# Group 8 of the tokens loaded as seven tokens on each of 64 partitions per sequence, and the unread matmuls of the drain left out

## The chip, the core and the metric

The kernel runs on one core of a Trainium2 chip. Five engines work side by side: PE (TensorE, matrix products; its weight loads are listed as PEld), DVE (VectorE), ACT (ScalarE), POOL (GpSimd) and SP (SyncE, which here only issues transfers). Sixteen DMA engines move data between the chip's main memory and the on-chip memory of 128 partitions. The metric is the time on the device of one execution, in microseconds (us); lower is better.

## What is computed

Four sequences (B = 4) of S = 5056 tokens with D = 256 channels go through a gated recurrence, and its result goes through a mixture of 8 experts with 4 slots each (32 slots in all). From the reference:

```python
sig = 1.0 / (1.0 + np.exp(-f_logit))
f = lower_bound[None, None, :] + (1.0 - lower_bound[None, None, :]) * sig
i = 1.0 - f
for t in range(S):
    h = f[:, t] * h + i[:, t] * x[:, t]
    y[:, t] = h
...
logits = x @ phi                       # x is y, all 20224 tokens
d = exp(logits - logits.max(0)); d /= d.sum(0) + 1e-09
slot_input = (d.T @ x).reshape(E, S_per_e, D)
slot_out[e] = np.maximum(slot_input[e] @ w1[e], 0.0) @ w2[e]
c = exp(logits - logits.max(1)); c /= c.sum(1) + 1e-09
out = c @ slot_out
```

The inputs x and f_logit are 20.7 MB each, the weights w1 and w2 together 16.8 MB, the output 20.7 MB. Nothing of the output can be computed before every token has gone through the recurrence and every expert's weights are there, since the softmax d runs over all tokens.

## The kernel before

**Tiling.** Each sequence is cut into 10 groups of 512 tokens. Groups 0 to 7 and the last, 9, are full; group 8 (called `odd`) has the 448 tokens that are left between 4096 and 4544. A unit is one group of one sequence: 40 units, worked off in the order of n = 0 to 39 in one loop. Units 32 to 35 are group 8 of sequences 0 to 3, units 36 to 39 are group 9.

**A unit's way through the engines.**
1. `load(n)`: SP issues the transfers of f_logit and x into tiles `f_t` and `x_t`, of two units each ([128, 2, 4, 256] in 4-byte numbers). Each kind has three buffers, so a load waits until the tile of three pairs earlier has been read.
2. `gate(n)`: ACT computes the sigmoid of the pair's `f_t` into `s_t` (2-byte numbers).
3. `enter(n)`: POOL multiplies `s_t` and `x_t` into `u_t` (L252).
4. `s_to_channels` and `u_to_channels`: PE turns `s_t` and `u_t` so that channels lie on the partitions and tokens run along them. Two channels of 2 bytes travel as one 4-byte number, so a turn is a transpose by an identity matrix.
5. `decay`: ACT makes the factors `a` out of the turned s. `scan`: DVE runs the recurrence over the tokens (two scans a unit, L319), its start value taken from the same sequence's group before.
6. `to_tokens`, `keep_tokens`: PE turns h back to tokens on partitions, DVE or ACT copies it out. `logits`, `exps`, `weights_to_tokens`, `slots`: the products with phi, the exponentials and the sums into the 32 slots.

**How a group lies on partitions.** A load must give each partition a run of consecutive tokens, for then the run is one packet of the transfer. In the first groups a partition holds 4 tokens of a unit (4096 bytes). The units from 8 to 31 are `long`: a pair of them is two successive groups of one sequence, a partition holds 8 tokens in a row (8192 bytes), and partitions 0 to 63 hold the first group, 64 to 127 the second. Such a pair's u is turned by halves, by `half_to_channels` (L273: eight transposes of 64 partitions for each unit), which reads both u tiles.

Group 8 pairs two sequences. Its 448 tokens are 3 x 128 + 64: each sequence has 3 tokens on each of 128 partitions (`R3`), and the 64 tokens that remain of both sequences share a fourth column (`rest`), token by token, sequence 0 on the even partitions and 1 on the odd ones. So a load of a pair has three transfers for f_t and three for x_t: the column (L222, 128 packets of 1024 bytes) and two blocks (L226, 128 packets of 3072 bytes each). `to_channels` turns such a unit with one product that sorts even and odd partitions apart (L261) and three transposes (L264).

**The order of the work** is written out by hand in the loop over n: at even n, `load(n + 6)`; then `gate`, `enter(n + 3)`, `to_tokens(n - 1)`, `s_to_channels` of two units, `u_to_channels(n + 1)`, `scan(n)`. Each engine does its instructions in that order. POOL also issues the transfers of the weights, which convert them to 2 bytes (`load_w`, at the places that `W_AT` lists: one each at n = 9, 17, 25, 31, 32, two at 33, three at 34, six at 36), so each stands in POOL's queue behind the `enter` before it. The transfers are taken up by the sixteen DMA engines in the order of each queue.

**The drain.** After the loop come the last group's slots, then the slots' sums are copied out by DVE (`slot_sb`), turned by PE (`sin_ps`), scaled (`sin`) and sent through the experts. At two places, after `late_slots` and after the `sin_ps` products, the kernel has PE do matmuls whose results nobody reads: `spin` (two of 128x256) and `narrow` (ten of 32x256), each time 12. Then the experts' products follow, each as its weights land (L631, L670, L728), and the output is computed in blocks and stored.

Of the kernel before, what the change touches and what calls it, by code (L numbers as in the profile page):

```python
# [9 lines left out]
F32 = mybir.dt.float32  # L10
# [8 lines left out]
def kernel(  # L19
# [10 lines left out]
    nc = tc.nc  # L30
    B, S, D = x.shape
    E = moe_w1.shape[0]
    F = moe_w1.shape[2]
    NS = moe_phi.shape[1]
    SPE = NS // E
    P = 128
    DC = D // P
    FC = F // P
    R = 4
# [6 lines left out]
    def first(g):  # L46
        return g * G if g < n_grp - 1 else S - G

    def used(g):
        return first(g + 1) - first(g) if g < n_grp - 1 else G  # L50
# [2 lines left out]
        return used(g) // R  # L53

    odd = n_grp - 2
    R3 = used(odd) // P
    L = used(odd) - P * R3
    assert 2 * L == P

    wide_r = 4 * R  # L60
    n_blk = (S // (P * wide_r))
# [1 line left out]
    blocks.append((n_blk * P * wide_r, (S - n_blk * P * wide_r) // P))  # L63
    assert sum(P * n_r for _, n_r in blocks) + L == S


    consts = ctx.enter_context(tc.tile_pool(name="consts", bufs=1))
    ident_f = consts.tile([P, P], F32, name="ident_f")
# [52 lines left out]
    rrow = store.tile([P, n_grp * R, B], F32, name="rrow")  # L121
    left = store.tile([P, L, 2], BF16, name="left")
    nc.vector.memset(left, 0.0)
# [8 lines left out]
    w1_sb = [wts.tile([P, DC, F], BF16, name=f"w1_sb{e}") for e in range(E)]  # L132
# [14 lines left out]
                nc.gpsimd.dma_start(out=w2_sb[i - E][:, ds(f, k)], in_=w2_r[i - E][:, ds(f, k)])  # L147


    def spin(dst, k, w):  # L150
        for _ in range(k):
            nc.tensor.matmul(dst[:, ds(0, w)], w1_sb[0][:, 0, :P], w1_sb[0][:, 0, :w],
                             start=True, stop=True, skip_group_check=True)

    def narrow(dst, k):
        for i in range(k):
            nc.tensor.matmul(dst[ds(i % B * NS, NS), ds(0, D)], w1_sb[0][:, 0, ds(0, NS)],
                             w1_sb[0][:, 0, ds(0, D)], start=True, stop=True,
                             skip_group_check=True)

    W_AT = {9: 1, 17: 1, 25: 1, 31: 1, 32: 1, 33: 2, 34: 3, 36: 6}
    w_next = [0]
    ctx.enter_context(tc.manual_schedule())
# [4 lines left out]
    with tc.tile_pool(name="sp2", bufs=3) as sp2, \  # L168
# [9 lines left out]
        slot_bank = pslot.tile([P, 2, D], F32, name="slot_ps")  # L178
# [12 lines left out]
        xs, fs, sts, uts, pss, psus, hs, hps, hts, lgs, ets = ({} for _ in range(11))  # L191

        def long(n):
            return 2 * B <= n < n_unit - 2 * B

        def place(n):
            if long(n):
                t, j = divmod(n, 2 * B)
                return 2 * t + j % 2, j // 2
            return divmod(n, B)  # L200
# [9 lines left out]
        def load(n, k=2):  # L210
            for src, dst, tag in ((f_logit, fs, "f_t"), (x, xs, "x_t")):
                if n % 2 == 0:
                    dst[n // 2] = ld.tile([P, 2, R, D], F32, name=tag, tag=tag)
                t = dst[n // 2]
                if long(n):
                    g, b = place(n)
                    nc.sync.dma_start(
                        out=t.rearrange("p u r d -> p (u r) d"),
                        in_=src[b, ds(first(g), 2 * G)].rearrange("(p r) d -> p r d", r=2 * R))
                elif n // B == odd:  # L220
                    b, t0 = n % B, first(odd)
                    nc.sync.dma_start(  # L222
                        out=t[:, 0, R3],
                        in_=src[ds(b, 2), ds(t0 + P * R3, L)].rearrange("b t d -> t b d"))
                    for m in range(2):
                        nc.sync.dma_start(  # L226
                            out=t[:, m, ds(0, R3)],
                            in_=src[b + m, ds(t0, P * R3)].rearrange("(p r) d -> p r d", r=R3))
                else:
                    for m in range(n, n + k):  # L230
                        nc.sync.dma_start(out=t[:, ds(m % 2, 1)], in_=tokens(src, m, 1))  # L231

        def gate(n, k=2):
            if n % 2 == 0:
                sts[n // 2] = sp2.tile([P, 2, R, D], BF16, name="s_t", tag="s_t")
            s_t, f_t = sts[n // 2][:, ds(n % 2, k)], fs[n // 2][:, ds(n % 2, k)]
            if n // B == odd:
                m = (R + R3) * D
                s_t = s_t.rearrange("p u r d -> p (u r d)")[:, :m]
                f_t = f_t.rearrange("p u r d -> p (u r d)")[:, :m]  # L240
            nc.scalar.activation(s_t, f_t, ACT.Sigmoid, scale=-1.0)  # L241

        def enter(n):
            uts[n] = sup.tile([P, R, D], BF16, name="u_t", tag="u_t")
            s_t, x_t = sts[n // 2][:, n % 2], xs[n // 2][:, n % 2]
            if n == 0:
                for r in range(0, R, 2):
                    nc.vector.tensor_tensor(uts[n][:, ds(r, 2)], s_t[:, ds(r, 2)],
                                            x_t[:, ds(r, 2)], ALU.mult)
            else:  # L250
                r = R3 if n // B == odd and n % 2 else R
                nc.gpsimd.tensor_tensor(uts[n][:, :r], s_t[:, :r], x_t[:, :r], ALU.mult)  # L252

        def to_channels(n, ps, t, rest):
            t = t.bitcast(F32)
            if n // B == odd:
                flat = ps.rearrange("c p r -> c (p r)")
                sides = ident_f.rearrange("p (t u) -> p u t", u=2)
                v = flat[:, ds(0, P * R3)].rearrange("c (p r) -> c p r", r=R3)
                k = P * R3 - n % 2 * L  # L260
                nc.tensor.matmul(flat[:, ds(k, P)], rest.bitcast(F32), sides,  # L261
                                 is_transpose=True, start=True, stop=True)
                for r in range(R3):
                    nc.tensor.transpose(v[:, :, r], t[:, r], ident_f)  # L264
                return
            for r in range(R):
                nc.tensor.transpose(ps[:, :, r], t[:, r], ident_f)  # L267

        def half_to_channels(n, ps, t):
            k = ds(n % 2 * (P // 2), P // 2)  # L270
            v = ps.rearrange("c p r -> c (p r)").rearrange("c (p r) -> c p r", r=2 * R)
            for r in range(2 * R):
                nc.tensor.transpose(v[:, :, r], t(r)[k].bitcast(F32), ident_f[k, k])  # L273

        def s_to_channels(n):
            if n % 2 == 0:
                pss[n // 2] = psp.tile([P, 2, P, R], F32, name="sp", tag="sp")
            to_channels(n, pss[n // 2][:, n % 2], sts[n // 2][:, n % 2],
                        sts[n // 2][:, 0, R3])

        def u_to_channels(n):
            ps = psu.tile([P, P, R], F32, name="up", tag="up")
            if long(n):
                half_to_channels(n, ps, lambda r: uts[n - n % 2 + r // R][:, r % R])
            else:
                to_channels(n, ps, uts[n], uts[n - n % 2][:, R3])
            psus[n] = ps.rearrange("c p r -> c (p r)").bitcast(BF16).rearrange(
                "c (t o) -> c t o", o=DC)

# [116 lines left out]
        def left_over():  # L406
            for b in range(B):
                k = ds(b * NS, NS)
                nc.gpsimd.tensor_copy(left[k, :, b % 2], etall[k, ds(S - L, L)])

# [74 lines left out]
        for n in range(n_unit):  # L485
# [14 lines left out]
            else:  # L500
# [40 lines left out]
                if n == n_unit - 2:  # L541
                    tail = psp.tile([P, 2, G], F32, name="tail", tag="sp")
# [46 lines left out]
        late_weights()  # L589
        slots(odd)  # L590
        late_slots()
        spin(tail[:, 1], 2, D)
        narrow(tail[:, 1], 10)
        slot_sb = hpool.tile([P, G, DC], BF16, name="slot_sb", tag="h")
        slot_sb = slot_sb.rearrange("p t o -> p (t o)").bitcast(F32)[:, ds(0, D)]
        nc.vector.tensor_copy(slot_sb, slot_ps)
# [2 lines left out]
        for o in range(DC):  # L599
            nc.tensor.matmul(sin_ps[:, o], slot_v[:, o], rep[:, 0],  # L600
                             start=True, stop=True, skip_group_check=True)
        spin(slot_bank[:, 1], 2, D)
        narrow(slot_bank[:, 1], 10)

    with tc.tile_pool(name="ew", bufs=1) as ew, \
         tc.tile_pool(name="pm", bufs=2, space=PSUM) as pm, \
# [17 lines left out]
        for q in range(E // Q):  # L624
            hi = ew.tile([P, F], BF16, name=f"hi{q}")
            for k in range(2):
                hi_ps = (psu.tile([P, H], F32, name="hi_ps", tag="up") if q == 0 else
                         pbig.tile([P, H], F32, name="hi_ps", tag=f"hi_ps{k}"))
                for o in range(DC):
                    for j in range(Q):  # L630
                        nc.tensor.matmul(hi_ps[ds(j * NS, NS)], sin[:, o],  # L631
                                         w1_sb[q * Q + j][:, o, ds(k * H, H)],
                                         start=(o == 0), stop=(o == DC - 1),
                                         skip_group_check=True)
# [7 lines left out]
        for q in range(E // Q):  # L642
# [4 lines left out]
            if q == 0:  # L647
                nc.tensor.matmul(cs_ps, rep2, cs1, start=True, stop=True)
            k = Q if q == 0 else Q - 1
            s0 = q * Q * SPE  # L650
            src = ht_ps[:, :, ds(s0, SPE)]
            src = bass.AP(tensor=src.tensor, offset=src.offset,
                          ap=[list(src.ap[0]), [P, FC], [NS + SPE, k], [1, SPE]])
            dst = hid[:, :, q * Q, ds(s0, SPE)]
            dst = bass.AP(tensor=dst.tensor, offset=dst.offset,
                          ap=[list(dst.ap[0]), [(E - 1) * NS, FC], [NS + SPE, k], [1, SPE]])
# [6 lines left out]
            src = ht_ps[:, :, ds((Q - 1) * NS + s0, SPE)]  # L663
# [23 lines left out]
        for i in range(0, n_late, 2):  # L687
            g_ps = (pbig.tile([P, 2, 2, P], F32, name="g_ps", tag="hi_ps1") if i else
                    psu.tile([P, 2, 2, P], F32, name="g_ps", tag="up"))
            for k in range(2):  # L690
                nc.tensor.matmul(g_ps[:, k], hi_v[tail_b, FC - n_late + i + k], ex[tail_b],
                                 start=True, stop=True, skip_group_check=True)
# [21 lines left out]
        for i in range(len(blocks)):  # L714
            expert(Q + i)
            row_sums(i)
            if i < len(blocks) - 1:
                k = ds(i * wide_r, wide_r)
# [3 lines left out]
        k = len(blocks) - 1  # L722
# [3 lines left out]
        for fc in range(FC):  # L726
# [4 lines left out]
                             start=fc == FC - n_late,  # L731
                             stop=fc in (FC - n_late - 1, FC - 1),
                             skip_group_check=True)
# [152 lines left out]
```

## Time and profile before

| | |
|---|---|
| median of three runs | 197.56 us (197.46 to 197.95) |
| the profiled execution | 197.47 us, of which its span 195.7 us |
| busy, share of the span | PE 75%, DVE 73%, ACT 72%, POOL 52% |
| moved | 58.23 MB read, 20.71 MB written |
| DVE scans (L319) | 72 with a start value, 1252 ns each, and 8 without |
| POOL products (L252) | 39 of 2131 ns in the mean; two of 128x768, 1667 ns |
| turning u by halves (L273) | 192 transposes |
| weights to the chip (L137, L147) | 14 transfers of 512 KB into their own tiles, 11.0 us from issue to landing in the median; four more, of 512 to 128 KB, into a reused tile |

The page of the profile divides the span into 40 slices of 4.9 us and gives the busy tenths of each engine in each; the clock that PE was granted; and what the DMA engines moved. The recurrence fills the slices up to about 127 us, the experts follow up to 145 us, and the stores fill the rest. A share of DMA above 1 means that packets of two queues overlapped on an engine. An engine's idle time is put down to what ended it ("DMA f_t<-in_f_logit_dram 6.4": 6.4 us of waits that this load ended); the chain of waits follows the run back from its last instruction, at each step to what released it.

### The profile page before, as it was taken

What the parts mean: (1) busy time and instruction counts of PE and PEld (TensorE: products, weight loads), DVE (VectorE), ACT (ScalarE), POOL (GpSimd) and SP (SyncE); (2) the same over time, 40 slices, a digit from 0 to 9 for tenths busy, and PEclk for the clock granted to TensorE, in tenths of its full rate; (3) what the DMA queues carried; (4) which work ended last, traced back from release to release, by engine and by line L of the source; (5) the groups of instructions that cost most, each with busy time, mean ns of one, the idle gap of its engine ahead of it and who ended that gap; (6) DMA issues with size and microseconds to landing.
All of it is one profiled execution on the core that took longest, in us unless ns stands there. A gap on an engine that the chain in (4) does not pass through costs nothing.

```text
span 195.7 us, 3272 instructions
## 1 busy us (share of the span) xinstructions
PE 147.1 (75%) x1204; PEld 103.8 (53%) x1204; DVE 143.5 (73%) x185; ACT 141.4 (72%) x200; POOL 101.3 (52%) x78
## 2 busy tenths in 40 slices
PE   0688598897989979898997978996797999910000
PEld 0477478675767758665785857465564434300000
DVE  2669869989799999999999999442377998910000
ACT  3688688799799998899998798334089999940000
POOL 2589578874998688884969977280030000000000
PEclk9999889999999999999999999999999655555555
DMA  4999999999999999999999999999949999999994
GB/s 199 418 421 419 427 425 424 429 427 361 379 427 425 401 332 425 429 414 308 402 420 395 270 225 213 214 214 214 167 175 425 431 417 435 435 445 432 435 432 174
DMA packets 14161, 70.75 MB, mean 362 GB/s; under 512 B 1585, under 2 KB 2866, under 8 KB 10178
## 3 DMA queue, kind: packets, MB, share of 16 engines
q1 hardware_dynamic: 11520, 62.13, 76.4%
q0 software_dynamic: 2624, 8.42, 21.6%
q8 instruction: 9, 0.15, 0.3%
q14 instruction: 6, 0.05, 0.1%
q10 hardware_dynamic: 2, 0.00, 0.0%
HBM read 58.23 MB, written 20.71 MB: 403 GB/s over the span
## 4 chain that ended last, share of the span: by engine, by line
PE 24%; DMA 21%; DVE 15%; POOL 10%; ACT 9%; issue 6%; SPq 2%; POOLq 1%; ACTq 0%
DMA x_t<-in_x_dram 12%; DVE h L319 11%; DMA w_t<-in_moe_w_dram 10%; PE op L821 8%; POOL u_t L252 8%; ACT oc L762 5%; PE hp L332 4%; PE up L273 3%; PE sp L267 3%; DVE ht L351 3%; SPq L231 2%; PE slot_ps L189 2%; PE lg L365 1%; POOL w_sb L147 1%; ACT s_t L241 1%
## 5 line engine op out<-in xcount | busy, mean ns | idle before, releaser
L252 POOL TENSOR_TENSOR u_t<-s_t,x_t 128x1024 bf16<-128x1024 bf16 (+1 forms) x39 | 82.5, 2131 | 21.8 <-ACT s_t L241 15.1
L319 DVE TENSOR_TENSOR_SCAN h<-a,h,up 128x512 bf16<-128x512 f32 (+1 forms) x72 | 86.8, 1252 | 4.4 <-PE up L273 2.1
L241 ACT ACTIVATE s_t<-f_t 128x2048 bf16<-128x2048 f32 (+2 forms) x23 | 38.3, 1668 | 6.4 <-DMA f_t<-in_f_logit_dram 6.4
L332 PE MATMUL hp<-ident_f,h 128*128 128x128 f32 (+1 forms) x160 | 29.6, 309 | 8.0 <-DVE ht L351 6.0
L332 PEld LDWEIGHTS hp<-ident_f,h 128*128 128x128 f32 (+1 forms) x160 | 23.2, 207 | 19.1 <-DVE ht L351 12.4
L267 PE MATMUL sp<-ident_f,s_t 128*128 128x128 f32 x144 | 22.3, 300 | 5.6 <-ACT s_t L241 3.8
L301 ACT ACTIVATE a<-sp,lbs 128x1024 f32<-128x1024 bf16 x24 | 25.5, 1115 | 0.6 <-PE sp L267 0.6
L762 ACT ACTIVATE oc<-op,rrow 128x256 f32<-128x256 f32 x62 | 24.2, 551 | 0.1
L821 PE MATMUL op<-slot_bd,etall 64*128 64x512 bf16 x62 | 22.8, 570 | 0.6 <-POOL slot_bd L751 0.2
L267 PEld LDWEIGHTS sp<-ident_f,s_t 128*128 128x128 f32 x144 | 18.0, 154 | 7.7 <-ACT s_t L241 4.6
L308 ACT ACTIVATE a<-sp,lbs 128x512 f32<-128x512 bf16 (+2 forms) x22 | 17.9, 859 | 4.7 <-PE sp L267 4.3
L758 DVE TENSOR_TENSOR oc<-op,rrow 128x512 f32<-128x512 f32 x31 | 19.7, 685 | 1.6 <-PE op L821 1.5
L273 PE MATMUL up<-ident_f,u_t 64*128 64x64 f32 x192 | 17.8, 230 | 2.2 <-POOL u_t L252 2.1
L273 PEld LDWEIGHTS up<-ident_f,u_t 64*128 64x128 f32 x192 | 14.0, 138 | 6.2 <-POOL u_t L252 2.8
L189 PE MATMUL slot_ps<-rep,ident_f 128*128 128x256 f32 x52 | 16.7, 415 | 0.0
L821 PEld LDWEIGHTS <-etall 64*128 64x128 bf16 x62 | 9.1, 154 | 13.4 <-issue 8.0
L351 ACT COPY ht<-hp 128x512 f32<-128x512 f32 (+1 forms) x20 | 11.7, 583 | 3.5 <-PE hp L332 3.4
L351 DVE COPY ht<-hp 128x512 f32<-128x512 f32 (+1 forms) x20 | 13.3, 667 | 0.8 <-PE hp L332 0.8
L319 DVE TENSOR_TENSOR_SCAN h<-a,up 128x512 bf16<-128x512 f32 x8 | 9.3, 1209 | 2.4 <-PE up L267 2.4
L267 PE MATMUL up<-ident_f,u_t 128*128 128x128 f32 x48 | 9.4, 327 | 0.5 <-POOL u_t L252 0.5
L365 PE MATMUL lg<-h,phi 128*32 128x512 bf16 (+1 forms) x80 | 9.4, 389 | 0.3 <-ACT et L389 0.2
L189 PEld LDWEIGHTS slot_ps<-rep,ident_f 128*128 128x128 f32 x52 | 8.3, 194 | 1.6 <-issue 0.6
(127 smaller groups left out, 141.9 us busy)
## 6 DMA issues: line engine op xcount, KB each, us to landing
f_t<-in_f_logit_dram SPq DMA_DIRECT2D x12, 1024.0 KB, 12.3
x_t<-in_x_dram SPq DMA_DIRECT2D x12, 1024.0 KB, 12.0
out_dram<-oc SPq DMA_DIRECT2D x6, 2048.0 KB, 14.1
w_sb<-in_moe_w_dram POOLq DMA_DIRECT2D x14, 512.0 KB, 11.0
f_t<-in_f_logit_dram SPq DMA_DIRECT2D x12, 512.0 KB, 8.4
x_t<-in_x_dram SPq DMA_DIRECT2D x12, 512.0 KB, 9.9
out_dram<-oc SPq DMA_DIRECT2D x4, 896.0 KB, 6.4
out_dram<-ob SPq DMA_DIRECT2D x1, 2048.0 KB, 9.7
```

What stands on the lines that cost most here:

```text
L189: nc.tensor.matmul(slot_bank[:, 1], ident_f, wide_rep, start=False, stop=False, skip_group_check=True)
L241: nc.scalar.activation(s_t, f_t, ACT.Sigmoid, scale=-1.0)
L252: nc.gpsimd.tensor_tensor(uts[n][:, :r], s_t[:, :r], x_t[:, :r], ALU.mult)
L267: nc.tensor.transpose(ps[:, :, r], t[:, r], ident_f)
L273: nc.tensor.transpose(v[:, :, r], t(r)[k].bitcast(F32), ident_f[k, k])
L301: nc.scalar.activation(a, sp[:, :, :, :, o], ACT.Identity, scale=nomlb[:, ds(o, 1)], bias=1.0)
L319: nc.vector.tensor_tensor_scan(h[:, :T, o], decays[n // 2, o][:, n % 2, :T], up[:, :T, o], hs[number(g - 1, b)][:, ds(used(g - 1) - 1, 1), ...
L332: nc.tensor.transpose(hp[:n_p, r], hw[:, :n_p, r], ident_f)
L351: copy(hts[g][:n_p, b].rearrange("p r d -> p (r d)").bitcast(F32), hps.pop(n)[:n_p].rearrange("p r c -> p (r c)"))
L758: nc.vector.tensor_tensor(ob, op, scale.broadcast_to(list(ob.shape)), ALU.mult)
L762: nc.scalar.activation(ob[:, i], op[:, i], ACT.Copy, scale=scale[:, i])
L821: nc.tensor.matmul(op.rearrange("p u d -> p (u d)"), ew[:, :, r], slot_bd[ds(j * 2 * NS, 2 * NS)].rearrange("s u d -> s (u d)"), start=Tru ...
```

## The change

Group 8 is laid out in another way. A sequence's 448 tokens now lie as 7 tokens (`R7`) on each of 64 partitions (L = 64), the pair's first sequence on partitions 0 to 63 and its second on 64 to 127. A load of a pair has two transfers for f_t and two for x_t, each of 64 packets of 7168 bytes to half of the partitions. The sigmoid works on the same 7 columns of 128 partitions as before. The product of the pair is still cut into 4 columns for the first unit and 3 for the second, but a column now holds tokens of both sequences; so each unit's turn reads both u tiles. s and u of group 8 are turned by halves, with seven transposes of 64 partitions each. `to_channels` loses its special case. The functions `spin` and `narrow` and their four calls are gone.

```diff
     odd = n_grp - 2
-    R3 = used(odd) // P
-    L = used(odd) - P * R3
-    assert 2 * L == P
+    L = P // 2
+    R7 = used(odd) // L
+    assert used(odd) == L * R7 and R < R7 < 2 * R
...
                 elif n // B == odd:
-                    b, t0 = n % B, first(odd)
-                    nc.sync.dma_start(
-                        out=t[:, 0, R3],
-                        in_=src[ds(b, 2), ds(t0 + P * R3, L)].rearrange("b t d -> t b d"))
                     for m in range(2):
                         nc.sync.dma_start(
-                            out=t[:, m, ds(0, R3)],
-                            in_=src[b + m, ds(t0, P * R3)].rearrange("(p r) d -> p r d", r=R3))
+                            out=t[ds(m * L, L)].rearrange("p u r d -> p (u r d)")[:, ds(0, R7 * D)],
+                            in_=src[n % B + m, ds(first(odd), L * R7)].rearrange(
+                                "(p r) d -> p (r d)", r=R7))
...
             if n // B == odd:
-                m = (R + R3) * D
+                m = R7 * D
...
-                r = R3 if n // B == odd and n % 2 else R
+                r = R7 - R if n // B == odd and n % 2 else R
...
-        def to_channels(n, ps, t, rest):
-            t = t.bitcast(F32)
-            if n // B == odd:
-                flat = ps.rearrange("c p r -> c (p r)")
-                sides = ident_f.rearrange("p (t u) -> p u t", u=2)
-                v = flat[:, ds(0, P * R3)].rearrange("c (p r) -> c p r", r=R3)
-                k = P * R3 - n % 2 * L
-                nc.tensor.matmul(flat[:, ds(k, P)], rest.bitcast(F32), sides,
-                                 is_transpose=True, start=True, stop=True)
-                for r in range(R3):
-                    nc.tensor.transpose(v[:, :, r], t[:, r], ident_f)
-                return
+        def to_channels(n, ps, t):
             for r in range(R):
-                nc.tensor.transpose(ps[:, :, r], t[:, r], ident_f)
-
-        def half_to_channels(n, ps, t):
-            k = ds(n % 2 * (P // 2), P // 2)
-            v = ps.rearrange("c p r -> c (p r)").rearrange("c (p r) -> c p r", r=2 * R)
-            for r in range(2 * R):
+                nc.tensor.transpose(ps[:, :, r], t(n % 2 * R + r).bitcast(F32), ident_f)
+
+        def half_to_channels(n, ps, t, n_r):
+            k = ds(n % 2 * L, L)
+            v = ps.rearrange("c p r -> c (p r)")[:, ds(0, L * n_r)].rearrange(
+                "c (p r) -> c p r", r=n_r)
+            for r in range(n_r):
                 nc.tensor.transpose(v[:, :, r], t(r)[k].bitcast(F32), ident_f[k, k])
...
-            to_channels(n, pss[n // 2][:, n % 2], sts[n // 2][:, n % 2],
-                        sts[n // 2][:, 0, R3])
+            ps, t = pss[n // 2][:, n % 2], lambda r: sts[n // 2][:, r // R, r % R]
+            if n // B == odd:
+                half_to_channels(n, ps, t, R7)
+            else:
+                to_channels(n, ps, t)
...
-            if long(n):
-                half_to_channels(n, ps, lambda r: uts[n - n % 2 + r // R][:, r % R])
+            t = lambda r: uts[n - n % 2 + r // R][:, r % R]
+            if long(n) or n // B == odd:
+                half_to_channels(n, ps, t, 2 * R if long(n) else R7)
             else:
-                to_channels(n, ps, uts[n], uts[n - n % 2][:, R3])
+                to_channels(n, ps, t)
...
         late_slots()
-        spin(tail[:, 1], 2, D)
-        narrow(tail[:, 1], 10)
...
                              start=True, stop=True, skip_group_check=True)
-        spin(slot_bank[:, 1], 2, D)
-        narrow(slot_bank[:, 1], 10)
```

The definitions of `spin` and `narrow`, taken out as well, are not shown.

## The prediction

> **What bounds the kernel now.** I read the 40 slices of the page first, then the busy time by stage, the chain of waits, and last the DMA issues and the trace's record of every DMA packet.
>
> ```profile
> PEclk9999889999999999999999999999999655555555
> DMA  4999999999999999999999999999949999999994
> GB/s 199 418 421 419 427 425 424 429 427 361 379 427 425 401 332 425 429 414 308 402 420 395 270 225 213 214 214 214 167 175 425 431 417 435 435 445 432 435 432 174
> ```
> The sixteen DMA engines are full in every slice but the first, one near 145 us and the last. The drop to 213 GB/s from slice 22 on is the expert weights: they are read as 4-byte and counted as written, 2-byte numbers, so 213 written is 426 read. The busy time by stage says the same (stretch and its length; busy us and count on PE, PEld, DVE, ACT, POOL; then PE's granted clock, DMA share, GB/s):
>
> ```profile
> 84.00:100.00 16.00, 14.68 (x147) 11.25 (x144) 15.62 (x16) 15.61 (x16) 12.56 (x7) 1.00 1.04 380
> 100.00:139.50 39.50, 33.19 (x387) 24.57 (x386) 28.09 (x36) 24.88 (x35) 23.82 (x27) 1.00 1.06 258
> 139.50:145.00 5.50, 5.36 (x50) 4.22 (x50) 3.15 (x8) 2.42 (x7) 1.76 (x2) 1.00 0.46 96
> 145.00:193.00 48.00, 25.62 (x80) 10.95 (x79) 24.46 (x40) 28.27 (x76) 0.07 (x1) 0.58 1.01 427
> ```
> So the run is one full DMA stream of loads up to 139.5 us, a turn of 5.5 us in which the experts' result is finished, and one full stream of stores. The chain of waits shows what ends the first part:
>
> ```profile
> 116.28 1.40 POOL u_t L252
> 117.68 0.70 issue
> 118.39 2.15 POOL w_sb L147 x4
> 120.54 18.94 DMA w_t<-in_moe_w_dram
> 139.48 0.04 issue
> 139.52 0.40 PE sum_ps L670 x8
> ```
> The last weights wait 18.9 us in the DMA queue, and PE starts when they land. Whatever adds a microsecond of DMA work before them adds one to the end; whatever delays an engine by less than the wait in the queue adds nothing. VectorE is nearly full too (15.62 of 16.00 us from 84 to 100), but is done with its scans at 123.1 us, 16 us before that landing.
>
> **Group 8's loads.** This is the term that decides. The issues of before:
>
> ```profile
> f_t<-in_f_logit_dram SPq DMA_DIRECT2D x4, 384.0 KB, 10.4
> x_t<-in_x_dram SPq DMA_DIRECT2D x4, 384.0 KB, 8.6
> ...
> f_t<-in_f_logit_dram SPq DMA_DIRECT2D x2, 128.0 KB, 10.0
> x_t<-in_x_dram SPq DMA_DIRECT2D x2, 128.0 KB, 9.4
> ```
> Eight issues of 384 KB are 1024 packets of 3072 bytes, four of 128 KB are 512 packets of 1024 bytes. The packet records give 122.9 ns and 46.5 ns as their means in this stage: (1024 x 122.9 + 512 x 46.5) / 16 engines = 9.35 us. After, the same 3.67 MB are eight issues, each of 64 packets of 7168 bytes, 512 in all, to 64 partitions. No load of this trace has that form, so I bound the packet.
>
> Low end: the stores of the 128x1792 output tiles have packets of 7168 bytes that took 272.6 ns, but over all 128 partitions. 512 x 272.6 / 16 = 8.72 us, and four issues fewer save 16 end marks of about 10 ns each on 16 engines, 0.04 us: 0.67 us less than before. High end: the slowest large packets written to the tiles are those of the weights, 4096 bytes in 323 ns, 12.7 bytes per ns; 7168 bytes would take 565 ns and the load 18.1 us, 8.7 us more than before.
>
> Between them I go by what rows of different kinds share. Loads of 8192 bytes ran at 26.4 bytes per ns and engine, stores of 7168 at 26.3 and of 16384 at 26.8: reading memory and writing it are different work, yet one ceiling holds both, so I put it on the side that both touch, the tiles' memory, as sixteen lanes of eight partitions. Each of these transfers covers 128 partitions. A transfer to 64 would have eight lanes for sixteen engines: 545 ns a packet, 17.44 us, and 8.05 us more than before with the marks. The two halves don't mend this by being issued together: each engine takes its share of the first before its share of the second, so all sixteen sit on one half at a time. Only engines out of step escape. The sixteen end marks of the last 1 MB load ahead of group 8 lie from 84.15 to 85.65 us, nine of them within 0.23 us: a leading engine has 1.5 us in hand before it becomes the last one. The cost lies between 8.05 - 1.5 = 6.55 and 8.05 us; since most engines are in step but the last four are far back, I take 6.7 us.
>
> The Trainium skill has a rule on just this (SBUF — State Buffer, section "Door 1: The DMA port swizzle"): partitions 0 to 63 reach only eight of sixteen ports, 196 GB/s measured at 1 MiB against 328 for all 128, and two transfers to the two halves at once gained 6%. No row here shows a load to half the partitions; by its two figures the load would take an estimated 328/196 x 8.72 = 14.6 us, and the sum would be 5.2 us instead of 6.7.
>
> **The rest.** *Turning.* For each sequence, s and u took one mixed matmul and three transposes, 0.11 + 0.33 us in the chain (L261, L264), and take seven half transposes now. Eight of that kind take 0.64 to 0.66 us (L273 x8), 0.081 each, so 0.57. Eight times 0.13 is 1.0 us more of PE between 98 and 110 us. The 14 to 19 us that weights wait in the queue hide it; without that cover it would cost its 1.0 us.
>
> *A new wait.* The first unit of a pair now reads both u tiles, so its turn waits for the second product too.
>
> ```profile
> 91.40 7.99 POOL L252 TENSOR_TENSOR u_t<-s_t,x_t 128x1024 bf16<-128x1024 bf16 x4 [2.81 <-ACT s_t L241]
> ...
> 101.85 0.28 PE L261 MATMUL up<-ident_f,u_t 128*128 128x128 f32 x1
> ```
> The four products of the first line include both of pair 32, done at 99.4 us; PE turns unit 32 from 101.7. For pair 34 it is 105.3 against 107.5. 2.2 us of margin each: nothing. If loads are late, products and turns go late together, behind them on PE the s of the next pair, then VectorE's scans; they may lose the same 6.7 us, as the weights land that much later. POOL issues the first weights after the product of unit 34, so these go late too, but group 9's eight loads of 1.25 us keep the queue full meanwhile.
>
> *Sigmoid, product, scan* keep their shapes: nothing. *SP* issues 8 transfers for 12 and waits for buffers anyhow: nothing.
>
> *The unread matmuls.* 24 of them run at 126.5 and 127.8 us, 0.39 + 0.51 + 0.38 + 0.51 = 1.8 us. The copy that PE waits for ends at 127.05 and the next matmul starts at 127.26, so they fill a wait; the second batch delays the first expert by 0.1 us at most, and PE then waits 0.9 us for each weight. Taking them out saves nothing.
>
> Sum, against the profiled execution's own 197.47 us (span 195.7 and 1.8 around it; median of the runs 197.56): 197.47 + 6.7 = **204.2 us**.
>
> **Rivals.**
> - *The lane goes with the engine, not with the partitions.* For it: the weights' packets write 12.7 bytes per ns but read 25.4, so there the ceiling isn't on the tiles' side. Then the load takes the low end: 197.5 - 0.67 = 196.8 us, faster, from the point on where sixteen engines on one half keep 272 ns a packet. Against: nothing but the equality of loads and stores. This is the other side.
> - *Engines fall out of step.* If the two that share a lane come to be a whole share apart (4 x 272.6 ns = 1.09 us), they alternate between halves and don't meet. Four of the engines lag by 1.3 to 1.5 us, for it; twelve lie within 0.8 us, against. About half the price: 197.5 + 3 = 200.5 us.
> - *PE's clock falls without the unread matmuls.* The one stretch of 3.41 us in which PE was busy for only a third was followed by one at half the clock (same columns):
>
> ```profile
> 19.59:23.00 3.41, 1.13 (x8) 0.70 (x6) 2.57 (x4) 2.99 (x3) 1.33 (x2) 1.00 1.04 429
> 23.00:26.41 3.41, 3.29 (x15) 3.21 (x16) 1.72 (x3) 1.35 (x3) 3.06 (x3) 0.50 1.03 435
> ...
> 125.40:128.81 3.41, 3.38 (x68) 1.92 (x69) 1.23 (x5) 0.29 (x1) 1.51 (x3) 1.00 1.05 210
> ```
> Without 1.8 us of them the last stretch keeps 1.6 of 3.4, still above that third, and stretches with 2.1 to 2.3 later kept the clock: against. If it falls all the same and stays down through the turn, PE's part of the chain there (139.52 to 142.55 us) doubles: 3 us, 197.5 - 0.7 + 3 = 199.8 us with full-speed loads. The Trainium skill (TensorE: Matmul & The Clock Gate, section "Part 1: The HAM clock gate") says the gate halves the clock after an idle window of about 3.4 us; the rows above agree with the 3.41 us step.
>
> **How the numbers follow.** Eight lanes for a half, 0.60 (its own range 203.0 to 206.2: 197.5 plus 5.5, where lagging engines save another microsecond, to plus 8.7); out of step 0.12; clock 0.05; lane with the engine 0.23. What this kernel's runs can tell from no change is about 0.3%, 0.6 us. The last case's gain of 0.67 lies right on that edge, and the extra microsecond of PE may eat some: 0.14 faster, 0.09 no change. The other three are slower, 0.77. The range goes from 196.6, a little under the low end, to 206.2, the high end of the packet.
>
> **What would show it.** Packets of 7168 bytes near 545 ns, not 272, in the load stage; a rate under 300 GB/s in the slices from 84 to 106 us with the DMA share still full; the last landing of w_t near 146 us; the turn from there to the stores still 5 to 6 us. Wrong if the packets stay at 272 ns, or if the weights land late because POOL issued them late with the queue empty.

## The result and the profile after

The changed kernel takes 206.03 us in the median of four runs (205.53 to 206.44) against 197.57 us (197.46 to 197.95): 1.0423 times the time before, with an interval of 1.0393 to 1.0452. It is 8.5 us slower, near the upper end of the range. The profiled execution took 206.44 us, its span is 204.6 us.

The page of the changed kernel: clock of PE in tenths, DMA share, and GB/s, in 40 slices of 5.1 us.

```profile
PEclk9999999999979999999997999999579755555555
DMA  6999999999999999999999999999919999999994
GB/s 207 424 416 420 431 429 421 432 412 328 426 424 426 352 392 428 424 186 247 267 233 411 317 255 215 214 211 216 195 20 382 429 417 458 410 455 416 426 445 211
```

In slices 17 to 20 (87 to 107 us) the DMA engines are as full as anywhere, but move 186 to 267 GB/s, where the slices of the kernel before moved 308 to 420 over the same time. That is where group 8 is loaded. Two more things differ towards the end: the clock drops to 5 in slice 28, and the gap before the stores (slice 29) is emptier than it was. The transfers of group 8 in the list of DMA issues (count, size, median us from issue to landing):

```profile
f_t<-in_f_logit_dram SPq DMA_DIRECT2D x4, 448.0 KB, 16.2
x_t<-in_x_dram SPq DMA_DIRECT2D x4, 448.0 KB, 15.8
```

They need 16 us to land where those of before needed 8.6 to 10.4. The chain of waits (start, length, what) now goes through these loads, and ends in PE:

```profile
91.33 16.57 DMA x_t<-in_x_dram
107.91 0.02 issue
107.92 15.86 DMA x_t<-in_x_dram
...
127.67 17.03 DMA w_sb<-in_moe_w_dram
144.70 0.04 issue
144.74 0.62 PE sum_ps L646 x6
145.35 1.87 PE tail L379 x16
...
151.54 0.23 PE sb_ps L704 x2
```

Between 79 and 124 us the chain holds nothing but these loads: the engines wait for x. The line at 145.35 is 16 small products; 16 of the same products took 1.21 us in the kernel before, at full clock. The chain leaves the weights at 144.70 us. The last of them land at 149.39, but PE comes to their products, the last line, only at 151.54, 2.2 us later; in the kernel before it came to them 0.6 us after they had landed. From 144.70 us on, PE at half clock is what ends late, and not the last landing.

Where the 9 us between the two profiled executions came from is read from the packet records: the end of the last weight packet, the start of the first store packet and the end of the last one.

| us | before | after | difference |
|---|---|---|---|
| start to last weight landed | 141.75 | 149.39 | +7.64 |
| the turn, to the first store | 2.53 | 4.11 | +1.58 |
| the stores | 49.70 | 49.58 | -0.11 |

Two causes, then: the loads end late, and the turn is longer. The busy time by stretches, first the turn of the kernel before, then the load stage and the turn of the changed one (stretch, length; busy us and count on PE, PEld, DVE, ACT, POOL; PE's granted clock, DMA share, GB/s):

```profile
141.80:144.30 2.50, 2.50 (x24) 2.17 (x23) 1.49 (x4) 1.73 (x5) 1.06 (x2) 1.00 0.04 9
```

```profile
84.00:107.00 23.00, 18.23 (x183) 13.71 (x181) 20.38 (x20) 17.55 (x18) 12.87 (x8) 0.99 1.03 258
149.40:153.50 4.10, 4.10 (x31) 3.17 (x29) 1.65 (x4) 1.72 (x5) 1.04 (x2) 0.81 0.01 4
```

The load stage of the kernel before, 84 to 100 us in the prediction's lines, had 380 GB/s at a DMA share of 1.04: the share is the same now, the rate is two thirds. In the turn PE is the whole time busy in both, with 24 matmuls at full clock before, with 31 at 0.81 after: it has more left to do when the last weight lands, and does it more slowly.

The packets of group 8 took 475.9 ns in the mean, against 272.6 for packets of the same size in the stores, with a wide spread (272 to 921; a quarter under 420, a quarter over 513). They come to 512 x 475.9 / 16 = 15.23 us instead of 9.35: 5.88 us more. Other loads got slower too. Group 9's packets of 4096 bytes, among and behind them, went from 161.4 to 179.4 ns in the mean (1.16 us), and those of 8192 bytes from 310.8 to 313.3 (0.48 us, nearly all of it after 84 us, beside group 8). The 4096-byte packets of the first 30 us, long before group 8 is loaded, went from 159.3 to 165.2 ns (0.75 us), which its loads can't have caused. Together that is 8.3 us of packet time for a landing that is 7.64 us later; where the difference went was not traced.

### The profile page after: what moved, and what is told of

Read it like the earlier page. It is cut to its first block, busy times and chain, and to the rows that moved or that the text cites. A ratio compares the mean times of both kernels' runs of the same rounds, so it can differ in the third digit from the quotient of the medians.

```text
span 204.6 us, 3267 instructions
## 1 busy us (share of the span) xinstructions
PE 149.6 (73%) x1204; PEld 105.1 (51%) x1204; DVE 144.1 (70%) x185; ACT 141.7 (69%) x200; POOL 101.3 (50%) x78
## 4 chain that ended last, share of the span: by engine, by line
DMA 43%; PE 16%; POOL 9%; ACT 9%; DVE 6%; issue 4%; POOLq 1%; ACTq 0%; SPq 0%; DVEq 0%
DMA x_t<-in_x_dram 35%; DMA w_sb<-in_moe_w_dram 8%; PE op L797 8%; POOL u_t L238 7%; ACT oc L738 5%; DVE h L299 5%; PE up L249 2%; PE hp L312 1%; PE tail L379 1%; PE sp L242 1%; ACT s_t L227 1%; DVE ht L331 1%; PE slot_ps L178 1%; POOL w_sb L147 1%; ACT L227 1%
## 5 line engine op out<-in xcount | busy, mean ns | idle before, releaser
L249 PE MATMUL up<-ident_f,u_t 64*128 64x64 f32 x220 | 21.0, 235 | 2.5 <-POOL u_t L238 2.5
L249 PEld LDWEIGHTS up<-ident_f,u_t 64*128 64x128 f32 x220 | 16.6, 143 | 7.2 <-POOL u_t L238 3.1
L178 PE MATMUL slot_ps<-rep,ident_f 128*128 128x256 f32 x52 | 17.2, 426 | 1.0 <-POOL rep L86 1.0
```

The lines of the kernel that those rows point to most:

```text
L178: nc.tensor.matmul(slot_bank[:, 1], ident_f, wide_rep, start=False, stop=False, skip_group_check=True)
```

## The experiments

Theory: loads to 64 partitions run on half of the lanes into the tiles' memory; the turn is longer because PE's clock halved. Rivals: turning by halves and waiting for both products cost; each transfer or each short one costs; the transfer needs only to be of 64 rows to be slow. Each time stands beside runs of the kernel before on the same chip.

**The layout alone: the changed kernel with the unread matmuls back.**

```diff
+        spin(tail[:, 1], 2, D)
+        narrow(tail[:, 1], 10)
...
+        spin(slot_bank[:, 1], 2, D)
+        narrow(slot_bank[:, 1], 10)
```

> The new layout of group 8 alone, with the unread matmuls back in the drain. Theory (eight lanes for sixteen engines, and besides a turn that ran at half clock because the unread matmuls are gone): the loads stay slow, 7168-byte packets near 476 ns and the last weight landing near 149.4 us, but the turn from there to the first store is 2.5 us again instead of 4.1: about 204.5 us. Rival (the clock fell because of where its 3.41 us steps lie once the loads end later, not for want of those matmuls): the turn stays at 3 to 4 us in some runs, 205.5 to 206.4 us.

Measured: 207.12 us (205.08 to 207.89, 1.0467 of before, interval 1.0404 to 1.0529). The packets took 504 ns, the last weight landed at 150.97 us, the turn took 4.01 us. So the layout alone makes the loss. The unread matmuls did not hold the clock here, which goes to the rival, though the median lies above both forecasts, for this time the loads were slower still. The stretches of 3.41 us by which the clock moved, first two of the changed kernel, then three of this run (columns as above):

```profile
140.72:144.14 3.42, 1.62 (x25) 1.38 (x25) 0.24 (x1) 0.96 (x2) 0.00 (x0) 1.00 1.07 214
144.14:147.55 3.41, 2.81 (x32) 1.97 (x31) 0.62 (x2) 0.00 (x0) 0.00 (x0) 0.50 1.05 200
```

```profile
141.99:145.40 3.41, 1.89 (x28) 1.47 (x27) 0.00 (x0) 1.07 (x2) 0.00 (x0) 1.00 1.08 217
145.40:148.82 3.42, 2.51 (x29) 1.94 (x32) 0.56 (x1) 0.00 (x0) 0.00 (x0) 0.50 1.05 196
148.82:152.23 3.41, 3.31 (x23) 2.34 (x24) 1.34 (x4) 0.00 (x0) 0.00 (x0) 0.50 0.27 46
```

A stretch in which PE waited for weights and was busy for 1.89 us (1.62 in the changed kernel) is followed by two at half clock, and these cover the first part of the turn.

**The matmuls alone: the kernel before without them.** The edit is the four calls taken out.

> The kernel before with only the 24 unread matmuls left out. Theory that their absence lowers PE's clock in the turn: the turn grows from 2.5 to about 4 us, 199.1 us. Rival that they matter only by chance or not at all: 197.5 us, clock full up to 152 us.

Measured: 198.87 us (198.53 to 200.37, 1.0059, interval 1.0038 to 1.0081). The last weight landed at 141.84 us, as before, but the turn took 3.89 us. Two stretches of the kernel before, and then three of this run:

```profile
132.23:135.64 3.41, 2.32 (x50) 1.81 (x43) 0.76 (x3) 1.87 (x4) 0.00 (x0) 1.00 1.06 215
135.64:139.05 3.41, 2.11 (x34) 1.81 (x32) 0.92 (x2) 0.00 (x0) 0.00 (x0) 1.00 1.05 208
```

```profile
132.28:135.69 3.41, 1.99 (x41) 1.50 (x30) 0.61 (x3) 1.63 (x3) 0.00 (x0) 1.00 1.05 213
135.69:139.10 3.41, 2.64 (x30) 2.08 (x28) 0.56 (x1) 0.00 (x0) 0.00 (x0) 0.50 1.06 208
139.10:142.52 3.42, 3.32 (x27) 2.40 (x26) 1.34 (x4) 0.00 (x0) 0.00 (x0) 0.50 0.66 111
```

The theory holds: in the kernel before, their absence costs about 1.2 us by the ratio of the runs, and the turn of the profiled execution is 1.4 us longer, at half clock. (That execution took 200.08 us, more than the median, since its stores were 1.2 us longer as well.) With them, the corresponding stretch has 2.32 us of PE and the next one 2.11, and neither was followed by half clock. The margin is thin: without them PE began the experts at 128.13 us instead of 128.34 and was done sooner with what it had, the next weights landed 0.1 us later, and so it waited 1.29 us for them instead of 0.96.

**The clock again: the changed kernel with PE kept busy where it waits for weights.**

```diff
         for i in range(len(blocks)):
+            if i < 2:
+                for _ in range(8):
+                    nc.tensor.matmul(tail[:, 1, ds(0, D)], w1_sb[0][:, 0, :P], w1_sb[0][:, 0, :D],
+                                     start=True, stop=True, skip_group_check=True)
             expert(Q + i)
```

> The changed kernel with eight unread matmuls of 128x256 ahead of each of the first two of the last experts, where PE waits for weights: so no stretch of 3.41 us there has PE busy for less than 2 us. Theory (of the loss, 1.6 us is PE's clock, which halves after a stretch with PE busy for 2.0 us or less, and the rest is the load): the last weight still lands near 149.4 us, the clock stays full, the turn is 2.5 to 2.8 us, 204.3 to 204.7 us. Rival (the longer turn has another cause, or the clock falls anyway): 205.5 to 206.5 us.

Measured: 205.63 us (204.90 to 206.36). The profile shows the turn (2.56 us) as expected, with the clock full, though the sixteen added matmuls are themselves part of the chain that ended last:

```profile
140.00:150.10 10.10, 9.08 (x132) 7.01 (x131) 2.89 (x10) 2.07 (x4) 0.00 (x0) 1.00 1.00 193
150.10:153.00 2.90, 2.90 (x27) 2.53 (x25) 1.89 (x4) 2.02 (x6) 1.40 (x2) 1.00 0.10 33
```

But the last weight landed at 150.13 us, since the packets of group 8 took 488.7 ns this time, and the median is only 0.4 us under the changed kernel's. The turn's cause is shown by the profile alone: the time of the whole is missed by 1 us and lies in the rival's range, for the loads' own spread from run to run covers most of the gain.

**The loads without the turning: the kernel before, its blocks loaded by halves.**

```diff
-                            out=t[:, m, ds(0, R3)],
-                            in_=src[b + m, ds(t0, P * R3)].rearrange("(p r) d -> p r d", r=R3))
+                        rows_m = src[b + m, ds(t0, P * R3)].rearrange("(p r) d -> p r d", r=R3)
+                        for p0, k in ((0, 64), (64, 64)):
+                            nc.sync.dma_start(out=t[ds(p0, k), m, ds(0, R3)],
+                                              in_=rows_m[ds(p0, k)])
```

> The kernel before, layout and turning kept, but each of group 8's blocks of 3072-byte packets loaded by two transfers, to partitions 0 to 63 and 64 to 127. Theory (eight lanes): the packets take 1.75 times as long as in the kernel before, as they did in the changed one (123 to about 214 ns), 5.9 us more of them and some of it again in the loads beside them, 203 to 205.5 us. Rival (the loss of the changed kernel comes from turning by halves and from the wait on both products): nothing of that is here, packets stay at 123 ns and the time at 197.5 us.

Measured: 204.85 us (204.41 to 205.34, 1.0368). The packets of 3072 bytes took 198.2 ns instead of 122.9, and those of 1024 bytes, to all partitions but in between, 70.1 instead of 46.5. The turning and the waits of the kernel before are untouched: the loss comes from the loads. The turn is 3.86 us here although the clock is full in it; PE came to the experts late (their first products at 138.7 us, 128.3 before), for the last x landed at 126.4 us, 11 us later than in the kernel before, more than the weights' wait in the queue could cover.

**The turning without slow loads: the two sequences woven.** This is the changed kernel with the unread matmuls back and one transfer for each tensor of a pair, over all 128 partitions.

```diff
-                    for m in range(2):
-                        nc.sync.dma_start(
-                            out=t[ds(m * L, L)].rearrange("p u r d -> p (u r d)")[:, ds(0, R7 * D)],
-                            in_=src[n % B + m, ds(first(odd), L * R7)].rearrange(
-                                "(p r) d -> p (r d)", r=R7))
+                    nc.sync.dma_start(
+                        out=t.rearrange("p u r d -> p (u r d)")[:, ds(0, R7 * D)],
+                        in_=src[ds(n % B, 2), ds(first(odd), L * R7)].rearrange(
+                            "b (p r) d -> p b (r d)", r=R7))
```

> The changed kernel's turning, product, waits and packets of 7168 bytes, with the unread matmuls back, but one transfer for each tensor of a pair: its 128 packets go to all 128 partitions, the two sequences on alternating partitions. The turn by halves is left as it is, so tokens of two sequences are mixed: the output of group 8 and what follows from it is not the reference's. Theory (only the transfers to half of the partitions cost): packets at 272 ns, last weight near 141.2 us, 196.9 us if the clock holds in the turn and 198.3 us if not. Rival (turning by halves and the wait on both products cost too): 199 us or more with packets at 272 ns.

Measured: 197.13 us (196.97 to 197.81 in ten runs), 0.9979 of before with an interval of 0.9967 to 0.9991. The same 512 packets of 7168 bytes took 275.9 ns, 8.83 us in all, and the last weight landed at 141.27 us:

```profile
f_t<-in_f_logit_dram SPq DMA_DIRECT2D x2, 896.0 KB, 12.5
x_t<-in_x_dram SPq DMA_DIRECT2D x2, 896.0 KB, 10.6
```

```profile
84.00:100.00 16.00, 14.68 (x149) 10.91 (x149) 15.60 (x16) 15.10 (x15) 12.49 (x7) 1.00 1.02 388
141.30:143.80 2.50, 2.50 (x24) 2.17 (x23) 1.50 (x4) 1.71 (x5) 1.03 (x2) 1.00 0.02 3
```

All else of the new layout, its 56 half transposes and the wait on both products, costs nothing that shows, and the longer, fewer transfers gain about 0.4 us. This is no finished kernel: it leaves out the sorting apart of the two sequences, so that its output is not the reference's. A way to do that was not run.

**Which part of the partitions.** The blocks of group 8 cut in three: partitions 32 to 95, which take 32 from each half, and the outer quarters. The edit is that of the run by halves with `((32, 64), (0, 32), (96, 32))`.

> As the run with halves, but the blocks are cut into partitions 32 to 95, 0 to 31 and 96 to 127. Theory (a lane belongs to partitions, and the two halves of 64 partitions have different lanes): the middle transfer reaches all sixteen lanes and is not slowed, only the two outer quarters are, so half of the loss of the run with halves: about 200.5 us, packets of two kinds, 123 and 200 to 250 ns. Rival (a transfer to 64 partitions or fewer costs more in itself, or each further transfer does): three transfers cost at least what two did, 203 us or more.

Measured: 207.99 us (207.14 to 209.54, 1.0536): the time went to the rival. The packets did not: 160.5 ns in the mean, half of them at most 121. But the DMA engines were not full:

```profile
84.00:107.00 23.00, 20.78 (x195) 15.81 (x194) 22.50 (x22) 18.58 (x19) 16.66 (x10) 1.00 0.89 278
```

With 28 transfers for group 8 instead of 12, the DMA share fell to 0.89 from the 1.04 of the run by halves in the same stretch; why was not tried apart. So the run decides nothing on lanes. The same two cuts on four loads of 1 MB, units 20 to 23, avoid small transfers:

```diff
...
+                    for p0, k in ((0, 64), (64, 64)) if n in (20, 22) else ((0, P),):
+                        nc.sync.dma_start(
+                            out=t[ds(p0, k)].rearrange("p u r d -> p (u r) d"), in_=rows_g[ds(p0, k)])
```

> The kernel before with four of its loads of 1 MB (units 20 to 23, packets of 8192 bytes) cut into transfers to partitions 0 to 63 and 64 to 127; group 8 untouched. Theory (eight lanes): 512 packets at 1.75 times 309 ns, 7.4 us more of DMA, 204 to 206 us. Rival (the loss needs something of group 8, as its place near the weights or its short packets): 197.5 us.

> As the run before it, but the same four loads are cut into partitions 32 to 95, 0 to 31 and 96 to 127. Theory (lanes belong to partitions, and 32 to 95 reach all of them): half of the bytes keep 309 ns, half go at 1.75 times that, 3.7 us more: 200.5 to 202 us. Rival (any transfer to 64 partitions or fewer is slow): as much as or more than the run with halves. With large transfers the number in flight should not bind, as it may have in the first run with a middle part.

Measured: by halves 208.37 us (207.88 to 208.83, 1.0546), the slow packets of 8192 bytes near 600 ns, and in the stretch of these loads, with the DMA share still full:

```profile
55.00:76.00 21.00, 17.19 (x146) 13.40 (x145) 17.71 (x18) 15.16 (x16) 13.41 (x8) 0.92 1.02 220
```

With a middle part 207.04 us (206.79 to 207.84, 1.0479) and packets near 560 ns. The first is more than expected (10.7 us later at the last weight instead of 7.4), and shows that group 8 is nothing special. The second misses: the middle part brought 2.6 us at the last weight, not half of the loss. To see one kind at a time, the next three runs added 2 MB of loads that nothing reads to the kernel before, at its units 18 and 20:

```diff
...
+        def extra(n):
+            rows = [f_logit[i, ds((n - 18) // 2 * G, G)].rearrange("(p r) d -> p (r d)", r=R)
+                    for i in range(B)]
+            for i in range(4):
+                nc.sync.dma_start(out=spare[(n - 18) // 2 * 4 + i][ds(p0, 64)],
+                                  in_=rows[i][ds(p0, 64)])
```

with 0 or 32 written for p0, and for the measure two transfers of all 128 rows in place of the four. The lines that name the spare tiles and call `extra` are not shown.

> The kernel before with 2 MB of extra loads, which nothing reads, in the middle of the recurrence: four transfers of 128 rows of 4096 bytes to all 128 partitions (into weight tiles that are filled later). Any theory: 512 packets of 4096 bytes at 159 ns, 5.1 us more of DMA, 202.6 us. It is the measure for the next two runs.

> The same 2 MB of extra loads as eight transfers of 64 rows of 4096 bytes, all to partitions 0 to 63. Theory (eight lanes for sixteen engines): 318 ns a packet, 10.2 us more, 207 to 208 us. Rival (the loss needs two halves that follow each other): 159 ns, 202.6 us.

> The same eight transfers of 64 rows, all to partitions 32 to 95, so that no transfer to another part is mixed in. Theory (lanes belong to partitions, 0 to 63 and 64 to 127 having eight each): all sixteen lanes are reached, 159 ns a packet, 202.6 to 203.5 us. Rival (any transfer of 64 rows is slow, whichever partitions it goes to): 318 ns, 207 to 208 us, as with partitions 0 to 63.

Measured:

| extra loads to | packet, mean ns | last weight landed, us | time, us |
|---|---|---|---|
| all 128 partitions | 159.3 | 147.21 | 202.94 (202.08 to 204.08) |
| 0 to 63 | 314.8 | 156.83 | 212.50 (211.20 to 212.64) |
| 32 to 95 | 159.5 | 146.76 | 203.40 (202.56 to 204.00) |

The packets and the landing are the fair measure: in the profiled executions of the first and the third, the clock fell ahead of the turn, which took 3.97 and 3.92 us; in the second it did not, and the turn took 2.53.

The stretch from 74 to 80 us, in the run to 0 to 63 and then in the run to 32 to 95:

```profile
74.00:80.00 6.00, 4.77 (x40) 3.76 (x36) 5.53 (x6) 1.75 (x3) 4.25 (x2) 1.00 1.04 219
```

```profile
74.00:80.00 6.00, 4.79 (x42) 3.76 (x36) 5.53 (x6) 2.92 (x4) 4.05 (x2) 1.00 1.02 423
```

This decides it. The same 64 rows, the same packets and the same number of transfers run at full rate to 32 to 95 and at half rate to 0 to 63. It is neither the number of rows nor the number of transfers, but which partitions they go to. The low ones came out dearer than expected (212.5, not 207 to 208): loads of 8192 bytes beside them were slowed as well, 328.8 ns against 310.9.

The last run, of a single execution, asks why a middle part among outer quarters was slow: transfers to 32 to 95 (4096-byte packets) and to 0 to 63 (2048-byte packets) in turn.

> The kernel before with extra loads that alternate: 64 rows of 4096 bytes to partitions 32 to 95, then 64 rows of 2048 bytes to partitions 0 to 63, four of each; the two kinds of packets can be told apart by size. The question is why cutting loads into a middle part and two outer quarters cost nearly as much as halves. Theory (engines are out of step, so one that is on the middle meets others that are still on the low half and share a lane with it): the 4096-byte packets are slowed too, to 200 ns or more in the mean, beside 2048-byte packets at 110 ns or more (84 alone). Rival (what goes to the middle is not slowed, whatever its neighbours are): 159 ns for the 4096-byte packets, and 150 to 168 ns for the others.

Measured: 204.92 us; 218.0 ns in the mean for the 4096-byte packets, 114.7 for the others. A quarter of the former kept 159 ns, a quarter took over 257. So a transfer that alone reaches all lanes is slowed by neighbours on half of them, as the theory of engines out of step has it. That it is such engines that meet is argued, not shown, since the records do not name a packet's engine.

## Why the prediction was right, step by step

**What bounds the kernel.** Right for the loads: the 7.64 us by which the last weight is late stand in full in the end, and the turn's own 1.58 us are added. (The landing at 139.5 us that the prediction calls the last is followed by three smaller ones, up to 141.75.) The room that PE and VectorE had was not unlimited, as the run by halves shows, where the last x came 11 us late.

**Group 8's loads.** The mechanism was right: sixteen engines on eight lanes. Of its reasoning, that equal rates of loads and stores put the ceiling on the tiles' side, the runs to 0 to 63 and 32 to 95 show the part that matters: the lane goes with the partitions. The Trainium skill (SBUF — State Buffer, section "Door 1: The DMA port swizzle") has this map: one bit of the partition's number picks between the two sets of eight ports, so 32 to 95 reach all. The trace agrees, at 219 and 423 GB/s. The size was made of two errors that nearly cancel, and so was in part luck. The packet was set at 545 ns and took 476: group 8 itself cost 5.9 us more, less than the 6.55 that the sum gave as its least. That engines out of step escape in part would explain it, but is not shown: the 1 MB loads cut by halves, also 64 packets to a transfer, took near 600 ns instead of 309, almost the full factor of two. The loads beside and behind group 8 lose too, 1.2 + 0.5 us, which the sum had at nothing. Predicted 6.7, measured 7.6.

**The other price.** The Trainium skill's 196 against 328 GB/s at 1 MiB gave 14.6 us for group 8's load, and 5.2 us for the sum. The load took 15.23 us, between that and the 16.0 that 6.7 us of cost stands for, and the last weight was 7.6 us late. In their stretch the 1 MB loads by halves moved 220 against some 420 GB/s, a ratio of 1.9, not 1.7; the measurement decides.

**Turning, the new wait, sigmoid, product, scan, SP.** Each was set at nothing, and the woven run bears it out for all of them together: 0.998 of before.

**The unread matmuls.** "Taking them out saves nothing" was right, and the sentence that rated them as mere fill was the step that failed: in the kernel before they hold the clock, at about 1.2 us. They put off the first expert by 0.2 us, not by 0.1 at most, and that little work, moved into the later wait, was enough to keep the clock. The sum set the turn at "still 5 to 6 us", counted from 139.5, that is, unchanged; it grew by 1.6. The rival with the clock had a chance of 0.05, on the ground that 1.6 us of PE in a stretch would be above the third (1.13 us) after which the clock had fallen. That bound was the error: 1.13 was the only fallen stretch that the profile had ahead of the stores, not the limit. Among stretches in which PE waited for weights, those with 1.62 (changed kernel), 1.89 and 1.99 us were followed by half clock as well, that with 2.11 was not. And the stretch that mattered was not the one with the matmuls, but one 7 us later, where PE waits for weights. In the changed kernel the clock fell with or without them. Where the stretches begin differs from one execution to the next (132.23 us in the profile before and 140.72 in the one after are 8.49 us apart, no multiple of 3.41), so which stretch comes out idle may be in part chance; that was not tried.

The whole, 6.7 + 0 predicted, 7.6 + 1.6 measured (less 0.1 in the stores and 0.2 behind the last of them), leaves the median, 206.03 us, just inside the likeliest case's own range, whose upper end was the slowest packet and not a fallen clock. That is luck: the range had no room set aside for the turn, and the profiled execution, 206.44 us, lies above it.

**The rivals.** Lane with the engine: refuted by the run to 0 to 63. Out of step: the spread of the packets and the run with both kinds agree with it in part, but the loss then spreads to the neighbours instead of being saved; that stays argued.

## What to carry to other kernels

Before a tile is cut by partitions, ask which partitions one transfer touches, not how many: a load to 0 to 63 runs at half rate, one to 32 to 95 or one that weaves two sources over all 128 does not, and two halves in one queue do not make up for each other. Longer packets are a small gain (here 0.4 us) that such a cut can turn into a loss nearly twenty times as large (here 7.6 us). Work whose result nobody reads may be there for PE's clock: look at how busy the stretches of 3.41 us ahead of the critical part are, not only at whether it fills a wait, and try it, since busy time alone did not tell which stretch was followed by half clock.

## What the hardware showed that was not expected

- Loads to all partitions are slowed by half-lane loads in the same queue: 46.5 to 70.1 ns for 1024-byte packets between halves, 310.9 to 328.8 ns for 8192-byte packets.
- Where PE waited for weights, stretches of 3.41 us with up to 2.03 us of PE (139.92 to 143.34 us in the run with a middle part on 1 MB loads) were followed by half clock, and the one with 2.11 us was not. No such limit holds elsewhere: in the changed kernel a stretch with 1.61 us (21.26 to 24.67 us) kept the clock, in the run with 1 MB loads by halves one with 2.50 us (38.62 to 42.03) lost it, and so did one with 2.68 us in the store stage of the kernel before (149.29 to 152.71). What the clock goes by beside the busy time stays open.
- With 28 transfers for the 3.67 MB of group 8 the DMA engines were no longer full (share 0.89); what limits them was not tried apart.
